# Seven block products for Q, K and V of two blocks, with weight sums made on the chip, in a float32 transformer block on Trainium2

## The chip, the cores and the metric

The kernel runs on one core of a Trainium2 chip. A core has a matrix engine (TensorE, PE), a vector engine (VectorE, DVE), a scalar engine (ScalarE, ACT), a general engine (GpSimd, POOL) and a queue engine (SyncE, SP) that here only issues transfers. Each engine works through its own instructions in order and waits at semaphores for the others. SBUF holds 128 partitions; PSUM, into which PE writes, has eight banks of 128 x 512 float32. The metric is the time of one execution on the device, in microseconds (us).

## The reference

One block of a transformer with two parallel branches, S = 2048 rows, D = 576, all in float32:

```
xn  = (x - mean(x)) / sqrt(var(x) + eps)
q, k, v = xn @ wqkv              # 32 heads of 18 columns
A   = softmax over 8 positions (t, t-2, ..., t-14) of q.k / sqrt(18), times v, then @ wo
B   = relu(xn @ w1 + b1)**2 @ w2 + b2        # 4608 hidden columns
out = x + A + B
```

## The kernel before

**Float32 as two parts.** PE multiplies a rounded float32 form (float32r). Each operand is split into a high part (ACT copies it to float32r) and a low part (DVE subtracts the high part from the original); a product is high x high + high x low + low x high. D = 576 is five chunks of 128 rows: four full ones, and one in which 64 rows hold the high part and 64 the low part of the last 64 columns, so this chunk needs two matmuls and not three: 4 x 3 + 2 = 14 matmuls for one product.

**Blocks and steps.** The 2048 rows are four blocks (b = 0 to 3) of TB = 512. Within a block a loop runs over NF = 36 chunks f of 128 hidden columns; n = 36 b + f counts the steps through the kernel, and n0 = 36 b is the first step of a block. A step (`step`, L669) loads the weights of step n+2 (`load_w`, L463, SP), splits W1 of n+1 (`split_w1`), runs what the table `pre` holds for n, then `ffn1` (L480: 14 matmuls of 512 columns, then ACT's Relu and two squares and DVE's `hl`), splits W2 (`split_w2`, L476), runs what `mid` holds, takes two pieces of side work, runs `ffn2` of step n-2 (`accumulate`, L511: 14 matmuls into the five banks of y) and takes a third piece. W2's low half in `split_out` (L123) is two DVE operations, of 512 and of 64 columns.

**Side work.** `side` is a list of generators: layernorm statistics and normalization of the next block, and the attentions. `attention` (L417) is for one block and one of G = 4 groups of 8 heads and is cut in 18 pieces, nearly all of them DVE operations over 128 x 1152 elements. It writes its result to DRAM and gathers it back in another order (`oscr`, `ob`); `o_chunk` and `o_acc` use that from n0+29 on.

**Q, K, V.** `load_wq` (L354) loads a group's weights in five chunks on SP and splits them; `qkv` (L405) multiplies them in four row tiles of 128 (`qkv_rows`, `three`, L366: 14 matmuls each), ACT copies the results out of PSUM (`qkv_out`, L390), and `qkv_close` (L397) stores K and V in DRAM (`kscr`, `vscr`) and reads the 14 rows in front of each partition's own (the halo) back from there. A group has 144 columns of K, 144 of V and a share of Q, `WIDE` columns in all: 512, 512, 384 and 320 in blocks 1 to 3; 448, 512, 384 and 384 in block 0. Blocks 1 to 3 do their groups at steps n0-2, n0+4, n0+11 and n0+18.

**Order and buffers.** In the opening and in the tail the order is written out by hand. Elsewhere a planner orders the instructions of each engine ahead of time by a model of their durations, the earlier in the program the more urgent, and sets the semaphores; on the chip this order is fixed. A tile name with bufs = k has k buffers in turn; a new use waits until the old one is done with. PSUM has five banks for y and three in turn (`wk`) for everything else. POOL makes only the powers of the layernorm (L147) and a few operations of the opening.

The functions that the change touches, as they were:

## Time and profile before

| | before |
|---|---|
| median of 3 runs | 1161.41 us (1161.28 to 1161.46) |
| the profiled execution's own time | 1161.42 us |
| its span, first to last instruction | 1159.7 us |
| PE busy, weight loads aside | 1154.3 us, 5227 matmuls |
| DVE, ACT, POOL busy | 847.5, 602.2, 18.3 us |
| moved by DMA | 185.90 MB, mean 160 GB/s |
| granted TensorE clock | full |

A row of a group of instructions reads: line, engine, operation, output<-input by the program's names, shape, xcount | busy us, mean ns of one | idle time of the engine in front of them, and what ended it. A row of the chain or of a timeline begins with start and length in us. A row of a list of waits reads: engine, tile and line that waited <- what it waited for: us in total, times, longest. A row of a table by stretches gives, after the stretch and its length, the busy time (and count) of PE, PE's weight loads, DVE, ACT and POOL, then PE's granted clock, the DMA engines' share and GB/s. A row of DMA issues ends with KB each and the us from issue to landing. Consecutive operations of an engine overlap a little, so durations of a group add up to slightly more than its busy time. Matmuls are pipelined: a row's mean of one (389 ns) is longer than the pitch from one to the next.

### The profile page before, as it was taken

The numbers are of one execution on the slowest core, as the hardware profiler recorded it, in microseconds if no ns is written. First come the engines' busy times: TensorE is split into PE (matmuls) and PEld (weight loads), VectorE is DVE, ScalarE is ACT, GpSimd is POOL, SyncE is SP. The second block draws the span as 40 slices with busy tenths as digits, with TensorE's granted clock in tenths as the row PEclk, the third lists the DMA queues.
The fourth block names the chain that finished last, engine by engine and source line by source line (L and its number), as shares of the span: only waits on it lengthen the run. The fifth ranks groups of instructions, "written<-read, shape, count | busy, mean of one in ns | idle before, by whom it ended". The sixth has DMA issues, their size and how long they took to land.

```text
span 1159.7 us, 14795 instructions
## 1 busy us (share of the span) xinstructions
PE 1154.3 (100%) x5227; PEld 966.5 (83%) x5227; DVE 847.5 (73%) x1373; ACT 602.2 (52%) x1086; POOL 18.3 (2%) x32
## 2 busy tenths in 40 slices
PE   9999999999999999999999999999999999999998
PEld 7888888888888888888888888888888888888887
DVE  6967798892788686995287969698528795957453
ACT  7645545563545454555364546555535455545552
POOL 2000000000000100000000010000000000000000
PEclk9999999999999999999999999999999999999999
DMA  8656547432656655444266665644326645353421
GB/s 290 214 170 223 177 133 234 123 112 63 209 190 206 212 183 198 132 115 120 63 234 203 203 216 153 214 111 125 106 75 232 221 131 184 108 181 111 121 63 51
DMA packets 89674, 185.90 MB, mean 160 GB/s; under 512 B 9984, under 2 KB 33280, under 8 KB 88320
## 3 DMA queue, kind: packets, MB, share of 16 engines
q1 hardware_dynamic: 89312, 184.58, 50.1%
q8 instruction: 41, 0.67, 0.2%
q10 hardware_dynamic: 288, 0.38, 0.1%
q14 instruction: 33, 0.27, 0.1%
HBM read 165.96 MB, written 18.96 MB: 159 GB/s over the span
## 4 chain that ended last, share of the span: by engine, by line
PE 99%; DMA 0%; DVE 0%; SPq 0%; issue 0%
PE y L515 44%; PE wk L492 39%; PE wk L372 14%; PE wk L236 1%; DMA xb<-in_x 0%; PE y L172 0%; PE wk L564 0%; DVE st L138 0%; DVE xr L566 0%; SPq L104 0%; DVE xt L166 0%
## 5 line engine op out<-in xcount | busy, mean ns | idle before, releaser
L515 PE MATMUL y<-hh,w2s 128*128 128x512 f32 x1292 | 319.8, 389 | 0.0
L515 PEld LDWEIGHTS y<-hh,w2s 128*128 128x128 f32 x1292 | 242.5, 188 | 50.4
L492 PE MATMUL wk<-xh,w1h 128*128 128x512 f32 x720 | 210.3, 389 | 0.0
L515 PE MATMUL y<-hl,w2s 128*128 128x512 f32 x718 | 189.5, 389 | 0.0
L492 PE MATMUL wk<-xh,w1l 128*128 128x512 f32 x720 | 187.6, 389 | 0.0
L120 DVE TENSOR_TENSOR w1l<-raw,w1h 128x640 fp32r<-128x640 f32 x144 | 118.1, 820 | 66.4 <-ACT w1h L118 52.0
L118 ACT ACTIVATE w1h<-raw 128x640 fp32r<-128x640 f32 x144 | 106.1, 737 | 115.7 <-PE wk L492 114.0
L124 ACT ACTIVATE w2s<-raw 128x576 fp32r<-128x576 f32 x144 | 97.8, 683 | 120.0 <-PE y L515 118.1
L492 PEld LDWEIGHTS wk<-xh,w1l 128*128 128x128 f32 x720 | 135.1, 188 | 28.1
L515 PEld LDWEIGHTS y<-hl,w2s 128*128 128x128 f32 x718 | 134.8, 188 | 28.0
L492 PEld LDWEIGHTS wk<-xh,w1h 128*128 128x128 f32 x720 | 134.9, 188 | 27.5
L492 PE MATMUL wk<-xl,w1h 128*128 128x512 f32 x576 | 154.1, 389 | 0.0
L126 DVE TENSOR_TENSOR w2s<-raw,w2s 128x512 fp32r<-128x512 f32 (+1 forms) x288 | 118.0, 453 | 47.3 <-ACT w2s L124 46.2
L499 DVE TENSOR_TENSOR hl<-r,hh 128x512 fp32r<-128x512 f32 x144 | 98.8, 686 | 42.4 <-ACT r L498 42.3
L492 PEld LDWEIGHTS wk<-xl,w1h 128*128 128x128 f32 x576 | 108.1, 188 | 22.6
L494 ACT ACTIVATE r<-wk,b1t 128x512 f32<-128x512 f32 x144 | 98.5, 684 | 39.7 <-PE wk L492 39.4
L425 DVE TENSOR_TENSOR pr<-qo,kv 128x1152 f32<-128x1152 f32 x64 | 86.6, 1353 | 34.7 <-DMA kv<-kscr 34.7
L372 PE MATMUL wk<-wqh,xh 128*128 128x512 f32 (+2 forms) x300 | 106.3, 355 | 0.0
L372 PE MATMUL wk<-wql,xh 128*128 128x512 f32 (+2 forms) x300 | 106.3, 355 | 0.0
L498 ACT ACTIVATE r<-r 128x512 f32<-128x512 f32 x144 | 91.0, 632 | 4.4
L497 ACT ACTIVATE hh<-r 128x512 fp32r<-128x512 f32 x144 | 90.9, 632 | 4.1
L447 DVE TENSOR_TENSOR pr<-lg,kv 128x1152 f32<-128x1152 f32 x64 | 86.8, 1356 | 1.6
(91 smaller groups left out, 961.1 us busy)
## 6 DMA issues: line engine op xcount, KB each, us to landing
raw<-in_w SPq DMA_DIRECT2D x144, 320.0 KB, 3.0
raw<-in_w SPq DMA_DIRECT2D x144, 288.0 KB, 2.8
kv<-kscr SPq DMA_DIRECT2D x16, 1008.0 KB, 5.7
kv<-vscr SPq DMA_DIRECT2D x16, 1008.0 KB, 8.2
wqr<-in_wqkv SPq DMA_DIRECT2D x35, 256.0 KB, 3.3
raw<-in_wo SPq DMA_DIRECT2D x20, 288.0 KB, 2.8
wqr<-in_wqkv SPq DMA_DIRECT2D x25, 192.0 KB, 4.0
kscr<-kv SPq DMA_DIRECT2D x16, 288.0 KB, 3.0
```

What stands on the lines that cost most here:

```text
L118: i = nc.scalar.activation(hi, raw, AF.Copy)
L120: i = nc.vector.tensor_tensor(out=lo, in0=raw, in1=hi.bitcast(F32), op=ALU.subtract)
L124: nc.scalar.activation(w[:, :D], raw, AF.Copy)
L126: nc.vector.tensor_tensor(out=w[:, o:o + n], in0=raw[:, a:a + n], in1=w[:, a:a + n].bitcast(F32), op=ALU.subtract)
L372: nc.tensor.matmul(ps, l, r, start=i == 0, stop=i == len(mm) - 1)
L447: nc.vector.tensor_tensor(out=pr.rearrange("p w (a d) -> p w a d", d=DH), in0=at[:, :, :, None].to_broadcast([P, W, HG, DH]), in1=shifted( ...
L492: nc.tensor.matmul(p, l, r, start=i == 0, stop=i == len(mm) - 1)
L494: nc.scalar.activation(r, p, AF.Relu, bias=b1t[:, f:f + 1])
L497: nc.scalar.activation(hh, r, AF.Square)
L498: nc.scalar.activation(r, r, AF.Square)
L499: last_hl[0] = nc.vector.tensor_tensor(out=hl, in0=r, in1=hh.bitcast(F32), op=ALU.subtract)
L515: nc.tensor.matmul(yp[b][c], v, a, start=first and c not in cs[:i], stop=c in last and c not in cs[i + 1:], skip_group_check=True)
```

## The change

**Seven products.** In blocks 2 and 3 the groups are taken in pairs, p = 0 of 2 x 512 columns and p = 1 of 2 x 352 (`PAIR`). Of the product of a block's rows with a pair's weights, the first four chunks of D are cut in 2 x 2: rows in two halves of 256, D in two halves of two chunks, columns in the pair's two groups. In place of eight products of a quarter with a quarter there are seven (the scheme of Strassen in Winograd's form) of sums and differences of quarters, which are added up to the four results. The fifth chunk is multiplied as before, within products 2, 7, 4 and 3 (`EXTRA`).

**Sums of weights.** They do not depend on the block. `preparation` makes them once, in blocks 0 and 1 (steps 6 to 12, 31 to 38, 40 to 46, 47 to 56, `PREP`), one in a step behind ACT's last square: POOL forms the difference in place and later the low half, ACT copies the high half, and POOL's queue stores both in DRAM (`wm`, `we`). The quarters come in by `load_quarter` on POOL's queue, each behind a one-column POOL copy.

**Sums of rows.** `sums` makes them on DVE from the normalized `xT` one step before the product, with ACT's copy for the high half, into the one buffer `sx`.

**Products.** `load_product` reads a product's weights, already split, on POOL's queue two steps ahead, into the buffers `wqh` and `wql` in turn; `multiply` runs 12 or 16 matmuls a product, at steps n0-6 to n0 and n0+3 to n0+9, into two banks `qk` that keep adding up over products 1 and 2; 6, 7 and 4; 5 and 3. DVE adds the results up in `cst` and `qo` (ACT copies those of products 1 and 2). K and V are stored after products 4 and 3, and `fetch` reads all of them back, halo and own rows, at n0+1, n0+6, n0+11 and n0+16, where the attention starts. The three PSUM banks are now one `wk` and two `qk`; an `ffn1` in a step with a product takes `wk`.

**The rest.** W2 and Wo lie with their last 64 columns in front as well, so that the low half is one operation of 576 columns and the high one of 640. Block 1 keeps the old way with block 0's widths. From step 19 on every odd step takes a fourth piece of side work. The loads of x, of its transpose and of the residual, and the layernorm, start at other steps; some tiles of the opening share buffers of later ones.

```diff
+DE = D + D - DM
...
-WIDE = [(448, 512, 384, 384)] + 3 * [(512, 512, 384, 320)]
-QAT = [[sum(n - 2 * CG for n in w[:g]) for g in range(G + 1)] for w in WIDE]
+WIDE = (448, 512, 384, 384)
+QAT = [sum(n - 2 * CG for n in WIDE[:g]) for g in range(G + 1)]
+PAIR = (512, 352)
+QP = (0, 448)
+PREP = {(0, 0): range(6, 13), (0, 1): (31, 32, 32, 33, 34, 34, 35, 37, 38, 38), (1, 0): range(40, 47), (1, 1): range(47, 57)}
+HOME = {(0, 0): "xr", (0, 1): "xb", (1, 0): "xr", (1, 1): "xt"}
+OUTS = {(0, 1): "xt"}
+LN, XT, NORM, RES = {1: 22, 2: 18, 3: 18}, {1: 25, 2: 13, 3: 14}, {1: 12, 2: 11, 3: 11}, {1: 20, 2: 13, 3: 13}
+PRODUCTS = {2: {0: range(-6, 1), 1: range(3, 10)}, 3: {0: range(-6, 1), 1: range(3, 10)}}
+FETCH = {2: ((0, 1), (1, 6), (2, 11), (3, 16)), 3: ((0, 1), (1, 6), (2, 11), (3, 16))}
+PLAIN = {1: ((0, -6, -2), (1, 1, 4), (2, 7, 10), (3, 13, 16))}
...
-    pw = ctx.enter_context(tc.tile_pool(name="pw", bufs=3, space=bass.MemoryType.PSUM))
+    pw = ctx.enter_context(tc.tile_pool(name="pw", bufs=1, space=bass.MemoryType.PSUM))
...
+    def bank(own=False):
+        turns[0] += not own
+        if own or turns[0] % 3 == 0:
+            return pw.tile([P, TB], F32, name="wk")
+        return pw.tile([P, TB], F32, name="qk", bufs=2)
...
     def split_out(w, raw):
-        nc.scalar.activation(w[:, :D], raw, AF.Copy)
-        for o, a, n in ((NC * P, 0, DM), (D, DM, D - DM)):
-            nc.vector.tensor_tensor(out=w[:, o:o + n], in0=raw[:, a:a + n], in1=w[:, a:a + n].bitcast(F32),
-                                    op=ALU.subtract)
-
-    ln, last_load, last_hl = {}, [None], [None]
+        nc.scalar.activation(w[:, :DE], raw, AF.Copy)
+        nc.vector.tensor_tensor(out=w[:, DE:], in0=raw[:, :D], in1=w[:, :D].bitcast(F32), op=ALU.subtract)
...
+    def minus(out, a, b):
+        nc.gpsimd.tensor_tensor(out=out, in0=a, in1=b, op=ALU.subtract)
+
+    def emit(raw, dst, n, rows):
+        outs[0] += 1
+        if rows is None:
+            o = mt.tile([P, 2, n], F32R, name=("wos", "sx")[outs[0] % 2], bufs=1)
+        else:
+            k = outs[0] % 2
+            o = rows[:, 2 * k * n:2 * (k + 1) * n].rearrange("p (k n) -> p k n", k=2).bitcast(F32R)
+        split(o[:, 0], o[:, 1], raw, nc.scalar)
+        minus(o[:, 1], raw, o[:, 0].bitcast(F32))
+        nc.gpsimd.dma_start(dst, o.bitcast(F32))
...
+    def load_quarter(p, m, c, h):
+        n = PAIR[p]
...
+        i = nc.gpsimd.tensor_copy(v[:, :1], gate[0][:, :1].bitcast(F32))
+        with tc.issue_after(i.ins):
+            nc.gpsimd.dma_start(v, wpair[p, :, c, h, :n])
...
+    def preparation(p, m):
+        b = lambda k, h: quarters[p, 2 * k + m, h]
+        n, rows = PAIR[p], None
+        if (p, m) in OUTS:
+            rows = sb.tile([P, NC, TB], F32, name=OUTS[p, m], bufs=1).rearrange("p c t -> p (c t)")
+        todo = [(1, (0, 0), None), (2, (1, 0), None), (3, (1, 1), None), (5, (0, 0), ((0, 1), (0, 0))),
+                (7, (0, 1), ((1, 1), (0, 1))), (6, (1, 1), ((1, 1), (0, 0))), (4, (1, 0), ((1, 0), (1, 1)))]
+        for i, w, terms in todo:
+            if terms:
+                minus(b(*w), b(*terms[0]), b(*terms[1]))
+            emit(b(*w), wm[p][i - 1][:, 2 * m:2 * m + 2], n, rows)
+            yield
+        if m:
+            r = [quarters[p, NC - 1, h] for h in range(2)]
+            for h in range(2):
+                emit(r[h], we[p][h], n, rows)
+                yield
...
+            minus(r[0], r[0], r[1])
+            emit(r[0], we[p][2], n, rows)
...
+    EXTRA = {2: 0, 7: 1, 4: 2, 3: 1}
+    mw, sx, qk, cst = {}, {}, {}, {}
+
+    def load_product(b, p, i, k):
+        n = PAIR[p]
+        t = mt.tile([P, NC, WQ], F32R, name=("wqh", "wql")[k % 2]).rearrange("p c t -> p (c t)")
+        w = t[:, :4 * n].rearrange("p (c t) -> p c t", c=4)
+        nc.gpsimd.dma_start(w, wm[p][i - 1])
+        hi = lo = None
+        if i in EXTRA:
+            hi = t[:, 4 * n:5 * n]
+            lo = sb.tile([P, n], F32R, name="wqr", bufs=2)
+            nc.gpsimd.dma_start(hi, we[p][EXTRA[i]][:, 0])
+            nc.gpsimd.dma_start(lo, we[p][EXTRA[i]][:, 1])
+        mw[i] = w, hi, lo
+
+    HALF = TB // 2
+
+    def sums(b, i):
+        v = lambda k, t: xT[b][:, 2 * k:2 * k + 2, t * HALF:(t + 1) * HALF]
+        s = sx[i] = mt.tile([P, 4, HALF], F32R, name="sx")
+        lo = s[:, 2:]
+        f = sb.tile([P, TB], F32, name="r", bufs=3).rearrange("p (c t) -> p c t", c=2)
+
+        def tt(out, a, b, op):
+            nc.vector.tensor_tensor(out=out, in0=a, in1=b, op=op)
+
+        if i == 7:
+            tt(f, v(0, 0), v(0, 1), ALU.subtract)
+        else:
+            tt(f, v(0, 1), v(1, 1), ALU.add)
+            if i != 5:
+                tt(f, f, v(0, 0), ALU.subtract)
+            if i == 3:
+                tt(f, v(1, 0), f, ALU.subtract)
+        nc.scalar.activation(s[:, :2], f, AF.Copy)
+        tt(lo, f, s[:, :2].bitcast(F32), ALU.subtract)
+
+    def result(b, p, t, row, col):
+        j = 2 * row + t
+        n = PAIR[p]
+        q = QP[p] + col * (n - 2 * CG)
+        return cst[b, p][:, col, :, j], qo[b][:, j, q:q + n - 2 * CG]
+
+    def halves(a, n):
+        return a[:, :2 * CG].rearrange("p (k c) -> p k c", k=2), a[:, 2 * CG:n]
+
+    def multiply(b, p, i):
+        n = PAIR[p]
+        if i == 1:
+            cst[b, p] = sb.tile([P, 2, 2, NJ, CG], F32, name="xb", bufs=1)
+            results(b)
+        w, ehi, elo = mw.pop(i)
+        s = sx.pop(i, None)
+        first = i in (1, 6, 5)
+        for t in range(2):
+            if first:
+                qk[t] = pw.tile([P, TB], F32, name="qk", bufs=2)
+            at = slice(t * P, (t + 1) * P)
+            if s is None:
+                k, row = {1: (0, 0), 2: (1, 0), 4: (1, 1)}[i]
+                js = slice(row * HALF + t * P, row * HALF + (t + 1) * P)
+                a = lambda m: (xh[b][:, 2 * k + m, js], xl[b][:, 2 * k + m, js])
+            else:
+                a = lambda m: (s[:, m, at], s[:, 2 + m, at])
+            mm = []
+            for m in range(2):
+                hi, lo = a(m)
+                mm += [(hi, w[:, 2 * m]), (hi, w[:, 2 * m + 1]), (lo, w[:, 2 * m])]
+            if i in EXTRA:
+                row = {2: 0, 7: 1, 4: 1, 3: 0}[i]
+                js = slice(row * HALF + t * P, row * HALF + (t + 1) * P)
+                mm += [(xh[b][:, NC - 1, js], ehi), (xh[b][:, NC - 1, js], elo)]
+            for c, (l, r) in enumerate(mm):
+                nc.tensor.matmul(qk[t][:, :n], l, r, start=first and c == 0, stop=c == len(mm) - 1,
+                                 skip_group_check=True)
+        for t in range(2):
+            src = halves(qk[t], n)
+            kept = result(b, p, t, 1, 0)
+            row, col = {1: (1, 0), 2: (0, 0), 6: (0, 1), 7: (1, 1), 4: (1, 0), 5: (1, 1), 3: (0, 1)}[i]
+            for o, a, u in zip(result(b, p, t, row, col), src, kept):
+                if i in (1, 2):
+                    nc.scalar.activation(o, a, AF.Copy)
+                else:
+                    nc.vector.tensor_tensor(out=o, in0=a, in1=u if i in (6, 7, 4) else o, op=ALU.add)
+        if i in (4, 3):
+            h = (4, 3).index(i)
+            for k, scr in enumerate((kscr, vscr)):
+                nc.sync.dma_start(flat(scr[2 * p + h], (PAD + b * TB) * CG, [NJ * CG, P], NJ * CG),
+                                  cst[b, p][:, h, k].rearrange("p j c -> p (j c)"))
+
+    def fetch(b, g):
+        kv[g] = tuple(mt.tile([P, NE, CG], F32, name="kv", bufs=3) for _ in range(2))
+        for t, scr in zip(kv[g], (kscr[g], vscr[g])):
+            nc.sync.dma_start(t.rearrange("p e c -> p (e c)"),
+                              flat(scr, (PAD + b * TB - HALO) * CG, [NJ * CG, P], NE * CG))
+        side.append(attention(b, g))
...
-        p = pw.tile([P, TB], F32, name="wk")
+        p = bank(own=n in held)
...
+    for (p, m), when in PREP.items():
+        at(mid, when[0], lambda p=p, m=m: prep.append(preparation(p, m)))
+        for k, n in enumerate(when):
+            at(mid, n, next_difference)
+            if k in (0, 1, 2, 3, 7, 8):
+                c, h = {0: (m, 0), 1: (2 + m, 0), 2: (2 + m, 1), 3: (m, 1), 7: (NC - 1, 0), 8: (NC - 1, 1)}[k]
+                after = when[k - 3] + 1 if k > 6 else 0
+                at(pre, max(n - 3, after), load_quarter, p, m, c, h)
...
-            at(pre, n0 - 26, load_x, b)
-            at(pre, n0 - 22, lambda b=b: side.insert(0, layernorm(b)))
-            at(pre, n0 - 12, lambda b=b: side.append(normalize(b)))
-            at(pre, n0 - 6, load_wq, b, 0)
-        at(pre, n0 + 13, load_residual, b)
-        if b:
-            at(pre, n0 - 2, start, b, 0)
-        for g, n in ((1, 4), (2, 11), (3, 18)) if b else ((1, 9), (2, 15), (3, 20)):
-            at(pre, n0 + n - 3, load_wq, b, g)
-            at(pre, n0 + n, start, b, g)
+            at(pre, n0 - 25, load_x, b)
+            at(pre, n0 - XT[b], load_xt, b)
+            at(pre, n0 - LN[b], lambda b=b: side.insert(0, layernorm(b)))
+            at(pre, n0 - NORM[b], lambda b=b: side.insert(0 if b > 1 else len(side), normalize(b)))
+            for p, when in PRODUCTS.get(b, {}).items():
+                for k, i in enumerate((1, 2, 6, 7, 4, 5, 3)):
+                    n = n0 + when[k]
+                    at(pre, n - 2, load_product, b, p, i, k)
+                    if i in (6, 7, 5, 3):
+                        at(mid, n - 1, sums, b, i)
+                    at(pre, n, multiply, b, p, i)
+                    held.add(n)
+            for g, n in FETCH.get(b, ()):
+                at(pre, n0 + n, fetch, b, g)
+            for g, l, n in PLAIN.get(b, ()):
+                at(pre, n0 + l, load_wq, b, g)
+                at(pre, n0 + n, start, b, g)
+            at(pre, n0 + RES[b], load_residual, b)
+        else:
+            at(pre, 20, load_residual, b)
+            for g, n in ((1, 9), (2, 15), (3, 20)):
+                at(pre, n - 3, load_wq, b, g)
+                at(pre, n, start, b, g)
...
             piece()
+            if n > 18 and n % 2:
+                piece()
```

## The prediction

> **What bounds the kernel now.** I read the page first, then the waits of TensorE (PE), then the chain in order of time. The page's engine rows and the chain's shares:

> ```profile
> span 1159.7 us, 14795 instructions
> PE 1154.3 (100%) x5227; PEld 966.5 (83%) x5227; DVE 847.5 (73%) x1373; ACT 602.2 (52%) x1086; POOL 18.3 (2%) x32
> ...
> PE 99%; DMA 0%; DVE 0%; SPq 0%; issue 0%
> ```

> PE is busy for 1154.3 of 1159.7 us and 99% of the chain. A busy PE need not be a PE at its peak, so the next view is all its waits:

> ```profile
> PE wk L621 <- DVE warm L614: 1.2, 1, 1.2
> PE wk L619 <- POOL rs L147: 0.6, 1, 0.6
> PE y L172 <- DVE xt L166: 0.2, 1, 0.2
> ```

> 2.0 us in all, every one in the opening. From there to the tail PE waits for nobody, so the time is a sum of matmul pitches: any matmul removed is worth its pitch, unless a new wait appears. The pitches come from the chain (start, length, count):

> ```profile
> 820.03 6.35 PE y L515 x28
> 901.85 12.24 PE wk L372 x54
> 958.52 9.73 PE wk L372 x56
> 1012.72 8.21 PE wk L372 x56
> ```

> 512 columns: 6.35/28 = 0.2268 us (12.24/54 gives the same); 384: 9.73/56 = 0.1738; 320: 8.21/56 = 0.1466 us. The 320- and 384-column pitches make 352 columns an estimate of 0.160. One step of the main loop (14 matmuls of ffn1, 14 of ffn2) is 28 x 0.2268 = 6.35 us.

> **The change part by part.** *PE.* Q, K, V of a block now: per group 4 row tiles x 14 matmuls = 56, so 56 x (0.2268 + 0.2268 + 0.1738 + 0.1466) = 43.3 us. After: a pair of groups takes seven products, each of 2 row tiles x 6 matmuls, and four of them carry 2 more per row tile for the fifth chunk: 84 + 16 = 100 matmuls where two groups had 112. At 512 and at 352 columns: 100 x (0.2268 + 0.160) = 38.7 us. That is 4.65 us less in each of blocks 2 and 3: **9.3 us**. Block 1 only moves 64 columns from a 512-column group to a 320-column one; between the pitches above 64 columns weigh 0.0266 to 0.0272 us, so its 56 matmuls of each kind gain and lose within 0.1 us: 0. All other matmuls keep number and width.

> *What hides the rest.* PE has only gaps to lose, so every other edit costs what it delays PE. Two covers matter, seen in the timelines of PE and DVE in block 2:

> ```profile
> 652.71 1.07 PE L492 MATMUL wk<-xh,w1h 128*128 128x512 f32 x4
> 655.88 2.20 PE L515 MATMUL y<-hh,w2s 128*128 128x512 f32 x9
> 668.58 2.20 PE L515 MATMUL y<-hh,w2s 128*128 128x512 f32 x9
> 670.62 1.29 PE L515 MATMUL y<-hl,w2s 128*128 128x512 f32 x5
> 656.14 0.82 DVE L120 TENSOR_TENSOR w1l<-raw,w1h 128x640 fp32r<-128x640 f32 x1 [1.26 <-ACT lg L438]
> 658.14 0.69 DVE L499 TENSOR_TENSOR hl<-r,hh 128x512 fp32r<-128x512 f32 x1
> 642.46 0.82 DVE L126 TENSOR_TENSOR w2s<-raw,w2s 128x512 fp32r<-128x512 f32 x2
> ```

> The ffn1 that starts at 652.71 gives the hl of 658.14, done at 658.83 and first read at 670.62, two steps on: 11.8 us of cover. The w1l of 656.14 goes into the buffer that the ffn1 ending at 655.88 has just left, for the ffn1 of 665.4, whose low part comes last (about 667.4): some 10.5 us. DVE may run about 10 us behind before PE feels it.

> *W2's low half.* A pair of 452 ns takes 0.82 us together; one 576-column operation lies between the 512- and 640-column rows (0.69, 0.82): 0.75. Less work for DVE, 54 ns more for ACT (640 for 576 columns); nothing on PE.

> *Sums and results on DVE, blocks 2 and 3.* Per pair eleven 128x512 operations (4 sums: 3, 2, 2, 4), and 5 products x 2 row tiles x 2 pieces of adding up. Rows for them, with the attention's, over block 2:

> ```profile
> L499 DVE TENSOR_TENSOR hl<-r,hh 128x512 fp32r<-128x512 f32 x36 | 24.7, 685 | 8.7 <-ACT r L498 8.7
> L447 DVE TENSOR_TENSOR pr<-lg,kv 128x1152 f32<-128x1152 f32 x16 | 21.7, 1356 | 0.4
> L425 DVE TENSOR_TENSOR pr<-qo,kv 128x1152 f32<-128x1152 f32 x16 | 21.6, 1352 | 8.6 <-DMA kv<-kscr 8.6
> L428 DVE TENSOR_REDUCE lg<-pr 128x64 f32<-128x1152 f32 x16 | 21.5, 1346 | 0.0
> L120 DVE TENSOR_TENSOR wql<-wqr,wqh 128x512 fp32r<-128x512 f32 (+2 forms) x20 | 11.8, 605 | 15.2 <-ACT wqh L118 15.1
> L451 DVE TENSOR_TENSOR pr<-pr 128x576 f32<-128x576 f32 x16 | 12.0, 752 | 0.1
> L452 DVE TENSOR_TENSOR pr<-pr 128x288 f32<-128x288 f32 x16 | 7.3, 456 | 0.4
> ```

> Sums: 22 x 0.69 = 15 us a block. Results: 20 of 288 columns at 0.456 and 20 smaller ones at about 0.3: 15 us. Gone: the splits of the weights, 11.8, and some 3 of W2. So 15 us more on DVE in a block, and the attentions are packed closer: from n0+2 to n0+22 (n0: a block's first step) 3 or 4 pieces a step take all four. In those 21 steps: fixed work 21 x (0.82 + 0.69 + 0.75) = 47; the attention, 84 in the rows above and some 13 in small ones, 97; pair 1's sums and results 14; together 158, and since consecutive operations overlap (two of 452 in 0.82) about 0.92 x 158 = 145 us, against PE's 21 x 6.35 + 16.0 = 149 us. DVE fits by a hair, at 97%. I cost it at nothing because of the 10 us of cover.

> *Sums in front of PE.* ACT's rows of the page, and one of PE's weight loads for later:

> ```profile
> L515 PEld LDWEIGHTS y<-hh,w2s 128*128 128x128 f32 x1292 | 242.5, 188 | 50.4
> ...
> L494 ACT ACTIVATE r<-wk,b1t 128x512 f32<-128x512 f32 x144 | 98.5, 684 | 39.7 <-PE wk L492 39.4
> ...
> L498 ACT ACTIVATE r<-r 128x512 f32<-128x512 f32 x144 | 91.0, 632 | 4.4
> ```

> sx has one buffer. The sums of products 7 and 3 can be written only when products 6 and 5 are done, and are read one step later: 6.35 us of cover for ACT's copy (0.63), DVE's low half (0.69), one piece in front of it (1.36) and ACT's Relu and two squares (0.68 + 2 x 0.63): 4.6 us. It fits; with another piece and an hl in front it is 6.7, 0.3 us too much, at 8 places: 2.6 us. Between 0 and 2.6 I take **0.9**, nearer to zero because PE shows no wait of this kind in 1,130 us. In those steps ffn1 has one PSUM bank in place of three; its Relu has a ffn2 and a product (3.2 + 1.9 us at the least) to come in, and needs 0.68.

> *Weight sums on POOL, blocks 0 and 1.* 34 low halves and 18 differences, 52 subtractions, half of 512 and half of 352 columns. POOL's rows and DVE's beside them in the opening, and DVE's load where they go:

> ```profile
> 11.26 1.16 POOL L203 TENSOR_TENSOR wql<-xr,wqh 128x448 fp32r<-128x448 f32 x1
> 8.44 0.62 DVE L203 TENSOR_TENSOR wql<-xr,wqh 128x448 fp32r<-128x448 f32 x1
> 11.93 1.54 DVE L203 TENSOR_TENSOR wql<-xr,wqh 128x448 fp32r<-128x448 f32 x2
> ...
> 53.00:115.00 62.00, 62.00 (x275) 51.33 (x274) 44.45 (x83) 29.85 (x55) 2.66 (x4) 1.00 0.60 192
> 315.00:380.00 65.00, 65.00 (x289) 53.81 (x288) 57.13 (x88) 33.33 (x60) 0.00 (x0) 1.00 0.61 205
> 380.00:445.00 65.00, 65.00 (x315) 56.42 (x314) 51.59 (x97) 31.75 (x64) 4.27 (x4) 1.00 0.53 171
> ```

> 448 columns take 1.16 us, so 1.32 for 512 and 0.91 for 352: 58 us, some 2 of each step's 6.35. The DVE pair that met the POOL subtraction at 11.93 took 1.54 us where two alone take about 1.16: it was held until POOL's end at 12.42. So I let all POOL time come off DVE's idle time. Steps 6 to 12: 11 x 1.32 = 14.5 us into 62.0 - 44.5 = 17.5 idle. Block 1 (315 to 445 us): 26 x 0.91 = 23.7 into 130 - 108.7 = 21.3. 2.4 us too much, inside the 10 us of cover: nothing.

> [...]

> *Queues.* SP loses 20 weight loads a block in blocks 2 and 3, and its waits for weight buffers with them; behind its K and V stores (which now wait for DVE's last add) stand the loads of W1 and W2, three buffers deep. POOL's queue issues 20 loads, 34 stores and 60 product loads; only POOL's own subtractions stand behind them. A product's load starts when product k-2 is done and has two ffn steps and a product, about 15 us:

> ```profile
> xt<-in_xt SPq DMA_DIRECT2D x3, 1280.0 KB, 8.0
> xr<-in_xt SPq DMA_DIRECT2D x4, 1024.0 KB, 4.9
> kv<-kscr SPq DMA_DIRECT2D x16, 1008.0 KB, 5.7
> ```

> 1 MB lands in 4.9 us, 1.25 MB in 8.0: covered by 7 us. No POOL load is in this trace; if it took twice 8.0 it would cost 1 us at each of some 24 products, and the other end is zero, since nothing waits for an early one. I take zero.

> **Sum.** The profiled execution's 1161.42 us (span 1159.7) - 9.3 + 0.9 = **1153.0 us**. The median of the runs, 1161.41, is the same.

> **The rivals.** *1. DVE becomes the bound of blocks 2 and 3 (slower).* All of K and V, not just a halo, now comes back from DRAM before an attention can begin. DVE waited 8.6 us for it in block 2, 2.2 for each attention. DVE's 145 us and four waits w must stay below 149 + 10 of cover: from w = 3.5 PE waits too, and from w = 4.7 the 4.65 us of a block are lost. With K's 5.7 us of landing in full: 145 + 23 - 159 = 9 a block, 18 in all, 1170 us. Against it: the fetch is issued about a step before the attention before it ends, and a third buffer is free for K.

> *2. POOL holds DVE (a part of the gain lost).* Odd steps now take a fourth piece, so in block 1's 18 steps 9 x 1.3 = 12 us of attention come earlier: 2.4 + 12 - 10 of cover = 4 us, 1157 us. Against it: the packed pieces are missing later, and one-input reductions are not held.

> *3. The products are not cheaper.* If a matmul of 352 columns were bound by its weight load (188 ns in the row above), pair 1 would take 18.8, not 16.0 us: 5.6 us back, 1158.6. Against it: 320 columns run at 146.6 ns with the same load.

> *4. Product loads come late (slower).* From 0.4 us each beyond the 15 us the gain is gone; at twice 8.0, which is 1 us too late 24 times, it is 24 us, 1177 us. Against it stand the landing times above.

> **How the numbers follow.** A measurement of this kernel tells about 0.2% (2.3 us) from no change. The forecast, 1151.5 to 1155.5: 0.60. Rival 2, with the milder end of rival 1, 1155.5 to 1159.1: 0.11; rival 3: 0.01. Rival 1 near w = 4.7, between 1159.1 and 1163.7: 0.07. Rival 1 beyond that 0.15, rival 4 0.06. So faster 0.72, the same 0.07, slower 0.21. The range goes from 1151.5 (the whole saving and half a microsecond) to 1164, which leaves out those 0.21. The forecast's own range is 1151.5 to 1155.5.

> **What would show it.** In the profile after: PE with 5179 matmuls or nearly, 48 fewer, and waits in its list of under 2 us beyond the opening; products of 12 or 16 matmuls at 0.2268 and about 0.160 us; DVE above 90% in the 21 steps of blocks 2 and 3; POOL some 75 us busy or more. A wait of PE for hl, w1l or sx in blocks 2 and 3 speaks for rival 1, in block 1 for rival 2, for wqh or wql on a DMA for rival 4. I am wrong if PE's sum of waits grows by more than 2.6 us.

## The result, and the profile after

The changed kernel takes 1154.63 us (median of 4 runs, 1153.23 to 1156.22) against 1161.35 us: a ratio of 0.9943, 95% interval 0.9925 to 0.996, or 6.7 us less. Another five runs of it gave 1154.32 us, 0.9935 (0.9922 to 0.9949). The forecast was 1153.0 us, with a range of its own from 1151.5 to 1155.5. The profiled execution is the longest of the four, 1156.22 us, with 2.8 us around its span; the others have 1.7.

The page of the kernel after: span, engines and the chain's shares.

```profile
span 1153.4 us, 14791 instructions
PE 1147.2 (99%) x5179; PEld 959.5 (83%) x5179; DVE 884.3 (77%) x1293; ACT 600.4 (52%) x1032; POOL 165.4 (14%) x218
...
PE 97%; DMA 2%; DVE 1%; ACT 0%; issue 0%; POOL 0%; ACTq 0%; POOLq 0%
```

PE has its 48 matmuls fewer and is the chain still, but 3% of the chain is now something else. The waits of PE (engine, tile, line <- what it waited for: us, times, longest):

```profile
PE y L697 <- DVE xr L713: 1.4, 1, 1.4
PE qk L803 <- DVE lg L796: 1.2, 1, 1.2
```

The second is the opening. The first is new: the first ffn2 of block 1 waits for DVE to empty block 0's banks of y. A wait is listed only from the modelled end of the last matmul on, so it costs a little more than it is long: this one of 1.4 us, some 2 by the starts of the matmuls around it, against a run without it. Nothing is listed for hl, w1l, sx, wqh or wql. The pitches, from the chain of the same kernel:

```profile
272.08 5.67 PE qk L394 x28
...
573.57 3.68 PE qk L569 x16
655.19 1.92 PE qk L569 x12
```

A product at 352 columns has 1.92/12 = 0.160 us a matmul, as estimated. At 512 columns it has 3.68/16 = 0.230, a little over the 0.2268 of the other matmuls, and block 1's 448 columns take 0.2025 where the pitches of 384 and 512 give 0.2003. If all 200 matmuls of products at 512 columns are as slow, these two add up to some 0.8 us (an estimate).

### The profile page after: what moved, and what is told of

It is laid out like the page before. It is cut to its first block, busy times and chain, and to the rows that moved or that the text cites. A ratio compares the mean times of both kernels' runs of the same rounds, so it can differ in the third digit from the quotient of the medians.

```text
span 1153.4 us, 14791 instructions
## 1 busy us (share of the span) xinstructions
PE 1147.2 (99%) x5179; PEld 959.5 (83%) x5179; DVE 884.3 (77%) x1293; ACT 600.4 (52%) x1032; POOL 165.4 (14%) x218
## 2 busy tenths in 40 slices
DMA packets 100490, 238.45 MB, mean 207 GB/s; under 512 B 13856, under 2 KB 37280, under 8 KB 95296
## 4 chain that ended last, share of the span: by engine, by line
PE 97%; DMA 2%; DVE 1%; ACT 0%; issue 0%; POOL 0%; ACTq 0%; POOLq 0%
PE y L697 44%; PE qk L672 20%; PE wk L672 18%; PE qk L569 7%; PE qk L394 4%; PE wk L394 2%; DMA wqr<-in_wqkv 1%; PE qk L257 1%; PE y L193 0%; PE wk L257 0%; DMA xb<-in_x 0%; DVE pr L605 0%; ACT wqh L141 0%; DVE lg L608 0%; ACT hh L677 0%
## 5 line engine op out<-in xcount | busy, mean ns | idle before, releaser
L147 ACT ACTIVATE w2s<-raw 128x640 fp32r<-128x640 f32 x144 | 105.6, 736 | 127.5 <-PE y L697 118.3
L148 DVE TENSOR_TENSOR w2s<-raw,w2s 128x576 fp32r<-128x576 f32 x144 | 114.4, 796 | 55.2 <-ACT w2s L147 54.8
L672 PE MATMUL qk<-xh,w1h 128*128 128x512 f32 x385 | 112.4, 389 | 0.0
L605 DVE TENSOR_TENSOR pr<-qo,kv 128x1152 f32<-128x1152 f32 x64 | 89.8, 1404 | 24.1 <-DMA kv<-kscr 18.5
L672 PE MATMUL qk<-xh,w1l 128*128 128x512 f32 x385 | 99.8, 389 | 0.0
L672 PE MATMUL wk<-xh,w1h 128*128 128x512 f32 x335 | 98.7, 390 | 0.0
L672 PE MATMUL wk<-xh,w1l 128*128 128x512 f32 x335 | 87.0, 389 | 0.0
L608 DVE TENSOR_REDUCE lg<-pr 128x64 f32<-128x1152 f32 x64 | 86.2, 1346 | 0.1
L672 PEld LDWEIGHTS qk<-xh,w1l 128*128 128x128 f32 x385 | 72.3, 188 | 15.1
L672 PEld LDWEIGHTS qk<-xh,w1h 128*128 128x128 f32 x385 | 72.2, 188 | 14.7
L672 PE MATMUL qk<-xl,w1h 128*128 128x512 f32 x308 | 82.4, 389 | 0.0
L672 PEld LDWEIGHTS wk<-xh,w1l 128*128 128x128 f32 x335 | 62.9, 188 | 13.1
## 6 DMA issues: line engine op xcount, KB each, us to landing
wqh<-wm POOLq DMA_DIRECT2D x8, 1024.0 KB, 6.2
kv<-kscr SPq DMA_DIRECT2D x8, 1008.0 KB, 5.8
kv<-vscr SPq DMA_DIRECT2D x8, 1008.0 KB, 9.2
wql<-wm POOLq DMA_DIRECT2D x6, 1024.0 KB, 5.2
```

The costliest lines, as they stand in the source:

```text
L147: nc.scalar.activation(w[:, :DE], raw, AF.Copy)
L148: nc.vector.tensor_tensor(out=w[:, DE:], in0=raw[:, :D], in1=w[:, :D].bitcast(F32), op=ALU.subtract)
L605: nc.vector.tensor_tensor(out=pr, in0=q[:, j:j + 1].to_broadcast([P, W, CG]), in1=shifted(k, j, [1, CG]), op=ALU.mult)
L608: nc.vector.tensor_reduce(out=lg[:, j * HG:(j + 1) * HG].rearrange("p a w -> p w a"), in_=pr.rearrange("p w (a d) -> p w a d", d=DH), axis ...
L672: nc.tensor.matmul(p, l, r, start=i == 0, stop=i == len(mm) - 1)
```

## The experiments

Each begins with what differs from the kernel after, or from the kernel before where that is said. With every edit the planner also orders the rest anew, so that two runs differ in their order as well as in the edit itself.

**The changed kernel again.** No edit.

> The changed kernel once more, to see what its spread consists of. Theory A (POOL's subtractions hold DVE, so that DVE's results come late in blocks 0 and 1): 1153.2 to 1156.2 us again; where the span is near 1151.6 PE has no wait after the opening, where it is near 1154 it has one or a few, of 1 to 3 us together, on something that DVE makes. Theory B (POOL's transfers lengthen the landing of block 1's weight chunks, and ACT stands behind them): the same times, and whenever PE waits a weight chunk took over 10 us to land just before.

1154.32 us. The wait at 320 us was gone from this profile, and another had come. DVE and then POOL and PE in block 1:

```profile
408.33 1.19 DVE L679 TENSOR_TENSOR hl<-r,hh 128x512 fp32r<-128x512 f32 x1
409.44 2.60 DVE L605 TENSOR_TENSOR pr<-qo,kv 128x1152 f32<-128x1152 f32 x1
411.96 1.50 DVE L148 TENSOR_TENSOR w2s<-raw,w2s 128x576 fp32r<-128x576 f32 x1
413.39 1.34 DVE L608 TENSOR_REDUCE lg<-pr 128x64 f32<-128x1152 f32 x1
414.65 0.81 DVE L143 TENSOR_TENSOR w1l<-raw,w1h 128x640 fp32r<-128x640 f32 x1
...
408.00 0.96 POOL L444 TENSOR_TENSOR sx<-xt,sx 128x352 fp32r<-128x352 f32 x1
409.86 2.99 POOL L444 TENSOR_TENSOR xt<-xt 128x352 f32<-128x352 f32 x2
...
422.54 1.43 PE L672 MATMUL wk<-xh,w1l 128*128 128x512 f32 x5 [0.34 <-DVE w1l L143]
```

In these rows, while POOL subtracts (L444), DVE's two-input operations are longer: hl 1.19 us (0.69 alone), the attention's product 2.60 (1.36), w2s 1.50 (0.75). The one-input reduction keeps its 1.34, also right beside a subtraction: in the kernel after, the one of 317.70 took 1.34 with POOL subtracting from 317.54 to 318.94. The w1l of 414.65 is done at 415.46, and PE begins to read it at 415.51. Its 10.5 us of cover are used up, and the one after it is too late by 0.34 us. Together with what is too short for the list, this stretch of block 1 cost PE 1.1 us (from 380.63 to 427.15 us, 46.5, where a run without a wait has 45.4).

**The subtractions on DVE.**

```diff
     def minus(out, a, b):
-        nc.gpsimd.tensor_tensor(out=out, in0=a, in1=b, op=ALU.subtract)
+        nc.vector.tensor_tensor(out=out, in0=a, in1=b, op=ALU.subtract)
```

> DVE makes the differences and low halves of the weight sums itself, 52 operations of 0.69 or about 0.52 us, in place of POOL; transfers, ACT and PE as in the changed kernel. Theory A: being held by a POOL operation of 1.0 to 1.6 us costs DVE more than doing it: PE's only wait goes, 1153.3 us with a spread under 0.5. Theory B: the transfers are as before, so is the wait: 1154.6 us with a spread of 3.

1153.61 us, 0.9937 (0.9925 to 0.995), span 1152.0. PE waits for nothing after the opening, though POOL's loads and stores are all still there: that speaks for A and against B, the transfers. Late weight chunks are there too. DVE's rows of this run:

```profile
311.26 0.69 DVE L143 TENSOR_TENSOR wql<-wqr,wqh 128x512 fp32r<-128x512 f32 x1 [1.86 <-ACT wqh L141]
408.74 0.56 DVE L143 TENSOR_TENSOR wql<-wqr,wqh 128x384 fp32r<-128x384 f32 x1 [5.85 <-ACT wqh L141]
```

DVE stands 1.86 and 5.85 us because ACT got a chunk late, and PE still does not wait. The times alone show less: the five runs go from 1153.23 to 1156.51 us, a spread of 3.3 where theory A had expected under 0.5. The longest was not the profiled one, and what it waited for is not known.

**No subtractions.** ACT makes a copy in place of each low half, and the differences are left out.

```diff
-        minus(o[:, 1], raw, o[:, 0].bitcast(F32))
+        nc.scalar.activation(o[:, 1], raw, AF.Copy)
...
-                minus(b(*w), b(*terms[0]), b(*terms[1]))
...
-            minus(r[0], r[0], r[1])
```

> The subtractions of the weight sums are left out (no differences; ACT copies the unsplit weights where POOL made the low half), so the products of blocks 2 and 3 are not those of the reference; loads and stores of the sums stay. Theory A: no hold of DVE is left, 1153.3 us with little spread. Theory B: the wait near 320 us stays, 1154.6 us.

1153.96 us (1153.5 to 1155.25), 0.9938 (0.9924 to 0.9951). No wait of PE after the opening; in the opening the profiled run, the longest, has 1.4 us of them more. The three pages' engine rows, without subtractions, with them on DVE, and (above) with them on POOL, tell more than the times:

```profile
PE 1147.6 (99%) x5179; PEld 961.2 (83%) x5179; DVE 852.6 (74%) x1293; ACT 617.7 (54%) x1066; POOL 92.1 (8%) x166
```

```profile
PE 1147.3 (100%) x5179; PEld 959.9 (83%) x5179; DVE 878.1 (76%) x1345; ACT 604.3 (52%) x1032; POOL 94.5 (8%) x166
```

52 subtractions make POOL 165.4 - 92.1 = 73.3 us busier, and DVE, which does none of them, 884.3 - 852.6 = 31.7 us busier. If DVE does all 52 itself, it is only 878.1 - 852.6 = 25.5 us busier. Giving them to POOL cost DVE more than doing them. Two more profiles say the same: 883.6 us of DVE in the repeated run, and 878.4 in a run below that also has them on DVE.

**The late order.** To make the effect large, the last seven sums of the first pair come at steps 39 to 42.

```diff
-PREP = {..., (0, 1): (31, 32, 32, 33, 34, 34, 35, 37, 38, 38), ...}
+PREP = {..., (0, 1): (31, 32, 32, 33, 39, 39, 40, 41, 42, 42), ...}
```

> The last seven weight sums of the first pair go from steps 34 to 38 to steps 39 to 42, away from the transfers of K, V and weight chunks at the seam of blocks 0 and 1. Theory A: the POOL work now meets a busier DVE, so the wait at the seam becomes one in block 1: 1154 to 1156 us. Theory B: the weight chunk lands in under 8 us, PE does not wait: 1153.3 us with a spread under 0.5.

1164.19 us (1159.11 to 1166.66, 11 runs), 1.0023 (1.0013 to 1.0033): 10 us, the whole gain, are lost, far more than either theory had expected. PE's waits in the profile, and PE's rows around the longest one:

```profile
PE qk L672 <- ACT w1h L141: 3.7, 1, 3.7
PE qk L672 <- DVE w1l L143: 1.3, 1, 1.3
PE wk L672 <- DVE w1l L143: 0.8, 1, 0.8
```

```profile
420.37 2.08 PE L672 MATMUL qk<-xh,w1h 128*128 128x512 f32 x4 [3.67 <-ACT w1h L141]
422.24 1.65 PE L672 MATMUL qk<-xl,w1h 128*128 128x512 f32 x4
```

Two were for DVE, as theory A has it. The longest was for ACT, which stood behind weight chunks (13.1 us for one, 4.4 for the next). So a third reading came up, C: the next block's x came late, and all that follows it. The next run tells.

**The late order, subtractions on DVE.** Both edits.

> The late order of the first pair's last seven weight sums (steps 39 to 42) is kept, and the subtractions run on DVE in place of POOL. With them on POOL this order took 1164.2 us, 10 us more than the kernel after. Theory A (POOL's subtractions hold DVE, so DVE's results come late in block 1): the 10 us go with them, 1153.5 to 1155.5 us. Theory C (the later sums keep the buffer of x, so the next block's x, its statistics and their round trip through DRAM come late, with DVE and ACT standing in order behind them): the delay stays, 1161 us or more, and the trace shows the same wait of DVE for x and of ACT for a weight chunk near 400 to 414 us.

1153.34 us (1153.14 to 1153.57), 0.9931 (0.9917 to 0.9946), span 1151.5, no wait of PE but the opening's. The order alone costs nothing. All 10 us need the subtractions on POOL, ACT's late chunk too: SP issued the load of x at 393.6 us in the late order, and at 383.4 us here. So C was a link in the chain, and not its start. Which wait of SP made the load late was not separated.

**The store of mean and power.** The late chunk leads to an edit of the change that the prediction does not mention. The layernorm's mean and power go to DRAM and come back spread over all partitions; they are now stored transposed, so that the two DVE operations of `normalize` read them without strides. Rows of before, then of after (transfers: count, KB, us to landing; the normalization):

```profile
mr<-mr SPq DMA_DIRECT2D x3, 4.0 KB, 1.4
L334 DVE TENSOR_TENSOR xt<-xt,mb 128x512 f32<-128x512 f32 x30 | 33.0, 1154 | 0.0
```

```profile
mr<-mr SPq DMA_DIRECT2D x3, 4.0 KB, 11.6
L355 DVE TENSOR_TENSOR xt<-xt,mb 128x512 f32<-128x512 f32 x30 | 19.1, 686 | 0.0
```

DVE gains 13.9 us in all; a store of 4 KB lands 10 us later. Theory D makes this store the cause of the late chunk. The edit, on the late order with POOL's subtractions:

```diff
-    mrscr = {b: dram.tile([2 * NJ, P], F32, name=f"mr{b}") for b in range(1, NB)}
+    mrscr = {b: dram.tile([P, 2 * NJ], F32, name=f"mr{b}") for b in range(1, NB)}
...
-        nc.sync.dma_start(mrscr[b].rearrange("n p -> p n"), mr.rearrange("p k j -> p (k j)"))
+        nc.sync.dma_start(mrscr[b], mr.rearrange("p k j -> p (k j)"))
```

(The tile `mb` and `normalize` take the strided layout again.)

> The late order of the first pair's last seven weight sums (1164.2 us, waits of PE of 9.5 us between 380 and 428 us) with the subtractions on POOL as they were, but the layernorm's mean and power stored to DRAM row by row as in the kernel before (landing 1.4 us), in place of transposed (11 to 14 us). Theory A (POOL's subtractions alone make DVE's results late): no change, 1161 to 1166 us. Theory D (the transposed store holds the transfer engines and SP's queue, so ACT gets its weight chunk late and w1h with it): the longest wait, 3.8 us for w1h, and the 1.7 us of half clock behind it go, while the 2.5 us of waits for w1l stay: 1157.5 to 1160 us. Against both it costs DVE some 4.6 us more for each block's normalization (687 to 1148 ns an operation), which lies before the next block.

1158.43 us (1157.16 to 1159.48), 0.9973 (0.9963 to 0.9983). ACT's second weight chunk, first in the late order and then with the store as before:

```profile
419.16 0.52 ACT L141 ACTIVATE wqh<-wqr 128x384 fp32r<-128x384 f32 x1 [4.37 <-DMA wqr<-in_wqkv]
```

```profile
414.45 0.53 ACT L141 ACTIVATE wqh<-wqr 128x384 fp32r<-128x384 f32 x1
```

It came 4.7 us earlier. PE's wait for w1h and what followed it are gone, while three waits for w1l, 3.9 us, stay. Here D holds, as an amplifier of A: the transposed store costs 1164.2 - 1158.4 = 5.8 us when A has already made everything late.

**That store alone undone, subtractions on POOL.**

> The kernel after with that one edit undone: mean and power stored row by row, and normalized with strides as before. Theory A: nothing changes for PE in block 1, 1154.5 +- 1 us; DVE is 14 us more busy in all. Theory D: block 1's thin margins (0.05 to 2 us for w1l near 415 to 422 us) grow, and the time goes to 1153.3 to 1153.7 us. If the normalization's 4.6 us more a block are what blocks 2 and 3 can't take: above 1156 us.

1155.11 us (1153.33 to 1158.03), 0.9949 (0.9932 to 0.9966). Nothing is won: PE still waits for w1l, 0.6 and 1.1 us at 415 and 423 us, and the times overlap with those of the kernel after. So nothing is seen there of D. DVE is busy for 900.5 us, 16 more, and PE has no wait in blocks 2 and 3.

**Both.**

> Subtractions on DVE and mean and power stored row by row. By PE's pitches alone, with no wait after the opening, the kernel after stands at 1153.3 us. Both theories: 1153.3 +- 0.5 us, no wait of PE behind the opening; it can't be faster than that, since PE does the same matmuls. Above 1155 us, DVE has too much to do in blocks 0 and 1 with some 40 us of subtractions and 14 us of normalization more.

1153.74 us (1153.3 to 1154.41), 0.9935 (0.9921 to 0.995), without a wait in block 1. It is no faster than the two kernels with the subtractions on DVE alone.

**Added work on DVE in blocks 2 and 3.** The subtraction for hl is done once or twice more than needed (`range(2 ...)`, `range(3 ...)`).

```diff
-        last_hl[0] = nc.vector.tensor_tensor(out=hl, in0=r, in1=hh.bitcast(F32), op=ALU.subtract)
+        for _ in range(2 if b > 1 and 2 <= f <= 22 else 1):
+            last_hl[0] = nc.vector.tensor_tensor(out=hl, in0=r, in1=hh.bitcast(F32), op=ALU.subtract)
```

> The subtraction that makes hl runs once more than needed, with the same result, in each of the 21 steps n0+2 to n0+22 of blocks 2 and 3: 2 x 21 operations of about 0.6 us more on DVE, 12 to 14 us a block. Cover theory (DVE may run some 10 us behind before PE feels it, and at 141 of 150 us it has 9 us left besides): 141 + 13 - 150 = 4 us behind at the end of the stretch, inside the cover: no change, 1154.5 +- 1.5 us, with hl done only about 5 to 8 us ahead of its first reader in place of 9 to 12. Rival (DVE is the bound of these blocks already): every added us is seen, 1154.5 + 2 x 13 = 1180 us.

1154.95 us (1154.25 to 1156.78), 0.9948 (0.9933 to 0.9962): no change.

> The same with two additional subtractions in each of these steps: 25 to 28 us a block. Cover theory: 141 + 26 - 150 = 17 us too much, 10 of them covered, some 6 to 8 us of PE's waits a block: 1166 to 1171 us, PE's waits standing at y for hl in the second half of the stretch. Rival (DVE is the bound already): 1154.5 + 2 x 26 = 1206 us. If DVE's pieces are held by something other than DVE's own work (the fetch of K and V, for example), the added work hides in these waits, and the time is under 1160 us.

1159.78 us (1158.01 to 1163.83), 0.9983 (0.9973 to 0.9992): about 5 us more than the kernel after, where the cover theory had some 12 to 16. By the number it is the last case, but not by its reason, since DVE has hardly any idle time in the stretch where the work was added. The tables by stretches, of the kernel after and of the one with two more, show where the added work went:

```profile
600.00:750.00 150.00, 150.00 (x691) 126.69 (x690) 140.98 (x222) 77.25 (x121) 12.59 (x21) 1.00 0.80 250
750.00:775.00 25.00, 25.00 (x112) 20.68 (x111) 17.80 (x27) 13.37 (x21) 0.00 (x0) 1.00 0.57 181
775.00:800.00 25.00, 25.00 (x112) 20.71 (x111) 17.43 (x27) 15.94 (x26) 0.00 (x0) 1.00 0.36 105
800.00:825.00 25.00, 25.00 (x112) 20.62 (x111) 10.06 (x15) 13.93 (x27) 2.16 (x4) 1.00 0.55 172
```

```profile
600.00:750.00 150.00, 150.00 (x691) 126.76 (x690) 143.93 (x237) 74.80 (x119) 12.75 (x21) 1.00 0.73 245
750.00:775.00 25.00, 25.00 (x112) 20.70 (x111) 24.23 (x33) 13.52 (x20) 0.00 (x0) 1.00 0.52 173
775.00:800.00 25.00, 25.00 (x112) 20.72 (x111) 22.89 (x37) 14.16 (x22) 0.00 (x0) 1.00 0.35 106
800.00:825.00 25.00, 21.69 (x91) 17.59 (x90) 15.04 (x23) 12.21 (x22) 0.57 (x1) 0.93 0.50 155
```

DVE's busy time (third of the engines) hardly grows in the 21 steps; it grows behind them. The planner kept the weights' low halves near their places (w1l at most 3.7 us later) and moved the attention back: block 2's last attention piece ends at 765.6 us in the kernel after, at 780.7 with one more and at 814.3 with two. PE feels it when the attention meets the next block's product 1, which writes the same `qo`. The chain of the profiled run with two more, its longest (1163.83 us):

```profile
813.94 0.32 DVE qo L633
...
814.28 7.63 DMA o<-qo
...
821.99 0.37 ACT qo L577
...
822.40 6.70 PE qk L569 x16
```

PE stood for 3.3 us in front of that product. In block 3, which has no next block, the same added work made no wait at all. (This run, 4 us above the median, also has waits of 1.5 and 1.1 us in blocks 0 and 1, where nothing was added.)

**The weight sums without their use.** All blocks from 1 on multiply as block 1 does; the sums are made and not read.

```diff
-PRODUCTS = {2: {...}, 3: {...}}
+PRODUCTS = {}
```

> Blocks 2 and 3 multiply by eight block products as block 1 does, with the weights as they come; the weight sums of blocks 0 and 1 are made and stored as in the kernel after, and nobody reads them. What it gives is the price of the preparation alone. Theory of the prediction (the preparation is hidden): PE has its 48 matmuls back, 1154.5 + 9.3 = 1163.8 us at most, 1161.3 to 1163.8 us. If the preparation costs more than the 1.8 us of wait seen near 319 us: above 1164 us. If the seven products gain more or less than 9.3 us in blocks 2 and 3, the difference to the kernel after is not 9.3 but says how much.

1166.09 us (1165.35 to 1169.7), 1.0047 (1.0032 to 1.0063): the case in which the preparation costs more. The profiled run, 1166.19, has these waits in block 1:

```profile
PE qk L672 <- ACT w1h L141: 2.0, 1, 2.0
PE qk L672 <- DVE w1l L143: 1.2, 1, 1.2
```

With what follows them they are 4.0 us; without them its span of 1164.5 would be 1160.5. Against the 1151.5 of the late order with DVE's subtractions, which has no wait there, the seven products are worth 9.0 us: worked out from two profiled runs, not run as a pair. In front of the wait of 2.0 us ACT stood 4.9 us for a weight chunk of 448 columns, which only a block's first group has, and which the kernel after does not load for block 2. So the preparation alone need not be the cause of all 4.0, and what made that chunk late was not separated. The preparation is not free, and its price hangs on the order that the planner finds: some 2 us in the profiled run of the kernel after, at most 4.0 here, 10 in the late order, nothing to be seen with the subtractions on DVE.

**W2's low half alone**, in the kernel before.

```diff
-        nc.scalar.activation(w[:, :D], raw, AF.Copy)
-        for o, a, n in ((NC * P, 0, DM), (D, DM, D - DM)):
...
+        nc.scalar.activation(w[:, :DE], raw, AF.Copy)
+        nc.vector.tensor_tensor(out=w[:, DE:], in0=raw[:, :D], in1=w[:, :D].bitcast(F32), op=ALU.subtract)
```

> The kernel before with one part of the change: W2 and Wo with their last 64 columns in front as well, and the low half of 576 columns as one operation in place of two. The prediction's step: 0.82 us of DVE for a pair become 0.75, 54 ns more on ACT, nothing on PE: 1161.3 +- 0.5 us. Rival (these operations are on PE's path): 144 x 0.07 = 10 us less, 1151 us.

1161.27 us, 0.9999 (0.999 to 1.0009): nothing, as forecast.

## Why the prediction was right

**The matmuls, -9.3 us: right.** 48 fewer, 352 columns at 0.160; 9.0 by the working above. The products at 512 columns are a little dearer (0.230 a matmul) than the 0.2268 of the sum. Rival 3 is out.

**W2's low half, 0: right**, by the run with it alone. A row of the new operation has 0.75 us.

**Sums in front of PE, 0.9 us: wrong place.** No wait for sx is listed. The 0.9 stood for a wait that did not come. Two other things came in its place: the kernels without a wait stand at about 1153.3 us, 1.2 above 1161.4 - 9.3, of which the pitches explain some 0.8, and the kernel after stands another 1.3 above that, which its profiles put down to POOL. That the sum came out within 1.6 us is in part luck.

**DVE in blocks 2 and 3, 0: right, for another reason.** It was busy for 141 of 150 us, 94%, close to the forecast 97%. But what gave way was not the 10 us in front of hl. It was the attention, up to the next block's product: some 13 us more a block (21 operations 0.61 apart) moved nothing, and twice that cost 5. Rival 1's sum was too harsh: 26 us more a block, put in place of its four waits, would have cost 141 + 26 - 159 = 8 us in each of the two blocks, and cost 5 in all. The wait itself was small too, as DVE's row for 560 to 1060 us shows:

```profile
DVE pr L605 <- DMA kv<-kscr: 2.2, 2, 1.3
```

**POOL's sums, 0: wrong, rival 2 in part.** The subtractions took POOL 73.3 us and not 58: 1.3 us for 512 columns as forecast where nothing is in the way, but one of 352 columns, 0.96 undisturbed, took 3.5 among DVE's operations. Not all of it came off DVE, but 31.7 us. The balance over whole blocks had taken off more, and called the 2.4 us that were too much covered. It failed locally: a held operation costs DVE 0.4 to 1.6 us in the profiled run, a few of them fall together, and where DVE has just stood for the next x or for a weight chunk, they meet a w1l or the emptying of y at its last moment. In the profiled run these rows stand before the 1.4 us:

```profile
311.38 0.69 DVE L143 TENSOR_TENSOR wql<-wqr,wqh 128x512 fp32r<-128x512 f32 x1 [1.82 <-ACT wqh L141]
314.48 1.34 POOL L444 TENSOR_TENSOR xt<-xb,xt 128x512 fp32r<-128x512 f32 x1 [12.46 <-ACT xt L141]
314.59 2.45 DVE L605 TENSOR_TENSOR pr<-qo,kv 128x1152 f32<-128x1152 f32 x1
319.67 1.41 DVE L713 SCALAR_TENSOR_TENSOR xr<-y,b2t,xr 128x512 f32<-128x512 f32 x2
320.47 0.73 PE L697 MATMUL y<-hh,w2s 128*128 128x512 f32 x2 [1.41 <-DVE xr L713]
```

It took both. In the repeated run the same operation is held as long, but DVE has not stood before it, and PE's y starts on time; with the subtractions on DVE it has stood (1.86 us, above), but nothing is held, and PE does not wait. The repeated run:

```profile
310.25 0.69 DVE L143 TENSOR_TENSOR wql<-wqr,wqh 128x512 fp32r<-128x512 f32 x1
313.46 2.45 DVE L605 TENSOR_TENSOR pr<-qo,kv 128x1152 f32<-128x1152 f32 x1
319.34 0.73 PE L697 MATMUL y<-hh,w2s 128*128 128x512 f32 x2
```

The place was the end of block 0 in the one run, and w1l in block 1 in the other; rival 2 had put 4 us there by earlier attention pieces, which was more than came. The L605 of 314.59 is done 1.22 us after POOL's end at 315.82, as if it had begun only there (alone it takes 1.35).

**Queues, 0: right for the products** (their 1 MB loads landed in 5.2 and 6.2 us in the median, 10.5 at the most, inside 15; rival 4 is out), **but a part of the change was left out**: the transposed store above. By the runs it cost nothing that the times show in the kernel after, and 5.8 us in the late order.

**What would show it.** 5179 matmuls, no wait for hl or sx and DVE above 90% were as said. POOL was busy for 165.4 us and not for some 75: besides the longer subtractions, its queue's 114 issues count there with some 63 us, 0.53 to 0.57 each. PE's listed waits went from 2.0 to 2.6 us in all, and past the opening from none to 1.4, less than the 2.6 that would have said wrong.

The kernel with the late order and DVE's subtractions, at 1153.34 us, is faster than the kernel before; its interval overlaps that of the kernel after, so the times alone do not part these two. Past the opening its profile has no wait of PE left.

## What to carry to other kernels

Two engines that hold each other, as DVE and POOL do here (the 52 subtractions made DVE 31.7 us busier when POOL did them, 25.5 when it did them itself), are not two engines for such work: compare what the second one takes off the first with what the first would need to do the work itself, operation by operation. A helper's load that fits over a whole stage can still miss its place within a step, so look for the thinnest margin and not for the sum. Where a planner orders the work, added work shows at whatever has the latest deadline; find that deadline before calling an engine the bound.

## What the runs showed of the hardware

**Pauses of PE.** The two longest pauses of PE, 3.3 and 3.7 us, cost more than their length. PE's clock in the stretches behind the longest waits, first of the run with two more subtractions and then of the late order (granted clock: third number from the end):

```profile
822.00:828.00 6.00, 5.60 (x13) 4.45 (x14) 1.31 (x2) 2.38 (x7) 0.00 (x0) 0.50 0.37 105
```

```profile
420.00:424.00 4.00, 3.63 (x10) 2.89 (x11) 4.00 (x5) 3.16 (x6) 1.73 (x4) 0.57 0.89 256
```

**Small packets.** The transposed store of 4 KB makes 1024 packets in place of 128: the page of the profile counts 13856 packets under 512 B in the kernel after and 11169 with that store undone, 2687 for three stores, some 896 each, which is 1024 - 128. In the kernel after, 6 to 11 us behind the issue of one such store at 403.0, the transfer engines were fully busy (a share of 1.21) at 138 GB/s, where they had moved 391 around the issue:

```profile
399.00:404.00 5.00, 5.00 (x24) 4.14 (x23) 3.85 (x5) 2.83 (x5) 3.69 (x7) 1.00 0.99 391
...
409.00:414.00 5.00, 5.00 (x24) 4.14 (x23) 5.00 (x6) 3.84 (x7) 1.95 (x1) 1.00 1.21 138
```

In the late order the same five microseconds (409 to 414) moved 263 GB/s with the transposed store, issued at 407.2, and 354 with the store as before, issued at 406.9. In the kernel after, the weight chunk that ACT waits for went into SP's queue just before the store, at 402.4, and landed at 410.1. How much of its time was the store's was not measured.
